# Turning the gathered rows of the last two experts on VectorE instead of TensorE in an attention and mixture-of-experts kernel

## The chip, the cores and the metric

The kernel runs on one core of one Trainium2 chip. A core has five engines that work side by side and wait for each other through semaphores: TensorE (PE in the profile; PEld is its weight load), VectorE (DVE), ScalarE (ACT), GpSimd (POOL) and SyncE (SP, which here only issues DMAs). Every engine takes its own instructions strictly in order. The metric is the time of one execution on the device in microseconds (us).

## What is computed

```python
# attention with a sigmoid: 8 batches, 12 heads, 448 tokens, 64 wide
scores = scale * np.matmul(q, k.transpose(0, 1, 3, 2)) - np.log(S)
x = np.matmul(1 / (1 + np.exp(-scores)), v)      # -> x: 3584 tokens x 768
# routing: each expert takes 448 tokens, by falling logit over all tokens and experts
logits = x @ w_gate                              # 3584 x 8
for idx in np.argsort(-logits.flatten()):
    tok, e = idx // E, idx % E
    if assigned[tok] >= 0 or counts[e] >= cap: continue
    assigned[tok] = e; counts[e] += 1
# experts: 768 -> 1024 -> 768
for e in range(E):
    h = np.maximum(x[mask] @ w1[e], 0.0)
    out[mask] = h @ w2[e]
```

All inputs and the output are float32.

## The kernel before

The program has two stages. In the first, attention is computed for 48 head pairs and the rows of x are stored to DRAM (`xs`). A row is not stored in the order of its 768 features. It is stored as four quarters of 192: quarter a holds, for each of the six blocks of 128 features, the 32 features that stand at place 32a to 32a+31 of the block.

In the second stage the eight experts run one after the other (`moe`). They are numbered here by the order in which the routing finishes them, 0 to 7. The first layer of an expert has four blocks of two weight units each, the second has three blocks of two, so an expert has 14 units; unit u of the whole program belongs to expert u // 14. TensorE multiplies in float32r, and each float32 operand is split in a high part, rounded by ScalarE (`xh`, `wh`, `hh`), and a low part that is the rest (`xl`, `wl`, `hl`). Three matmuls then replace one (lines 1000, 1002, 1004 in the first layer, 1037, 1039, 1041 in the second). An expert is 144 + 144 such matmuls of 448 columns; below they are counted 0 to 287.

Who makes the parts: ScalarE makes `wh` (L856) and GpSimd `wl` (L858), except that VectorE makes `wl` of the odd units from number 84 on. Of the first layer's output, ScalarE makes `hh` (L1008) and a plain copy into `yt` (L1011), and GpSimd makes `hl` from the two (L1012).

How x gets in: the 448 rows of an expert are gathered from `xs` by four indirect DMAs on the GpSimd queue (`gather`, L878, 128 rows each, the last 64). ScalarE puts each block of rows into the order of features (`order`, L887), and TensorE turns it by 24 small matmuls against the identity, in eight groups of three (`xturn`, L904). ScalarE and VectorE then make `xh` (L907) and `xl` (L908). This is done for an expert while the one before it runs.

The routing runs on VectorE (`Router`), one expert or two ahead of the matmuls. Its longest part is `grid_search`: nine rounds of three counts over a tile of keys (L321), each round needing the threshold `r_base` (L361) of the round before. After the ninth round TensorE turns `r_base` (L408) and sums the counts (L409), in line with its other matmuls. Then follow `place` (L452 to L461), `lists` (L481 to L496) and `remove`.

What sets the order: the program counts a clock of its own, 189 ns for each large matmul, and emits the other work between matmuls by due times on this clock. Each part of the routing has a time after which its next part is emitted, and `chores` is a list of due times with at most one chore per 1000 ns. Scatters of an expert's result (L956, on the GpSimd queue) and the stores and loads that bring the result into rows are chores as well. The engines then run freely in the order so written.

Of the kernel before, what the change touches and what calls it, by code (L numbers as in the profile page):

```python
# [7 lines left out]
F32 = mybir.dt.float32  # L8
F32R = mybir.dt.float32r
BF = mybir.dt.bfloat16  # L10
I32 = mybir.dt.int32
I16 = mybir.dt.int16
F16 = mybir.dt.float16
AF = mybir.ActivationFunctionType
OP = mybir.AluOpType
# [3 lines left out]
STEP = 4.0e36  # L19
BIG = 16384.0  # L20
TWO23 = float(2 ** 23)
XR_BUFS = 12
LATE = 1
XT_BUFS = 3
XZ_BUFS = 2
# [5 lines left out]
T_LATER = 1000  # L31
SLACK = 150
CHORE_NS = 1000
H_POOL = 8
EARLY = 1
FIRST = 4000.0
W_DVE = 84
Y_WAIT, Y_LATE = 5000, 26000
N_FAST = 9
PAD = 168  # L40
NONE = 1.0e30
FOUND, FOUND_ALL = 0x43E00000, 0x455FC800
# [14 lines left out]
def route_consts(nc, cp, K):  # L57

    K.G = cp.tile([128, 128], BF, name="c_G")
    ti = cp.tile([128, 128], I32, name="c_ti")  # L60
    nc.gpsimd.iota(ti, [[1, 128]], base=128, channel_multiplier=-1)
    t1 = cp.tile([128, 128], I32, name="c_t1")
    nc.gpsimd.iota(t1, [[1, 128]], base=0, channel_multiplier=0)
    t9 = cp.tile([128, 1], I32, name="c_t9")
    t10 = cp.tile([128, 1], F32, name="c_t10")
    nc.gpsimd.iota(t9, [[0, 1]], base=0, channel_multiplier=1)
    K.CN = cp.tile([128, 32], F32, name="c_CN")
    nc.gpsimd.memset(K.CN, 0.0)
    K.TRI = cp.tile([128, 128], BF, name="c_TRI")
    K.ones = cp.tile([128, 1], BF, name="c_ones")  # L70
    nc.gpsimd.memset(K.ones, 1.0)

    K.io64 = cp.tile([112, 64, 32], I16, name="c_io64")
    nc.gpsimd.iota(K.io64, [[1, 64], [0, 32]], base=0, channel_multiplier=0)
    K.io8 = cp.tile([112, 8], I16, name="c_io8")
    nc.gpsimd.iota(K.io8, [[1, 8]], base=0, channel_multiplier=0)

    K.rank = cp.tile([128, 8], F32, name="c_rank")
    t3 = cp.tile([128, 8], I32, name="c_t3")
    nc.gpsimd.iota(t3, [[-1, 8]], base=8, channel_multiplier=0)  # L80
# [12 lines left out]
    nc.gpsimd.iota(t6, [[1, 2], [2, 4]], base=0, channel_multiplier=0)

    K.kk = cp.tile([128, 16, 3], I32, name="c_kk")
    t8 = cp.tile([128, 3], I32, name="c_t8")
    nc.gpsimd.iota(t8, [[1, 3]], base=1, channel_multiplier=0)
    K.c0 = cp.tile([128, 3], I32, name="c_c0")
    for i, u in enumerate((0xBFFFFFFF, 0x00000000, 0x40000000)):
        nc.gpsimd.memset(K.c0[:, i:i + 1], _s32(u))  # L100
    yield
    yield
    nc.vector.tensor_scalar(t1, t1, 4, None, OP.logical_shift_right)
    nc.vector.tensor_scalar(t9, t9, 4, None, OP.logical_shift_right)
    nc.vector.tensor_copy(t10, t9)
    yield
    nc.vector.tensor_scalar(K.G, t1, t10, None, OP.is_equal)
    nc.vector.tensor_scalar(K.TRI, ti, 128.5, None, OP.is_gt)
    yield
    nc.vector.tensor_copy(K.rank, t3)  # L110
    nc.vector.tensor_copy(K.tok, t4)
    nc.vector.tensor_scalar(t5, t5, 31, None, OP.bitwise_and)
    t7 = cp.tile([128, 1], F32, name="c_t7")
    nc.vector.tensor_copy(t7, t5)
    yield
    nc.vector.tensor_scalar(K.SEL, t6, t7, None, OP.is_equal)
    g = 0
    for st in range(1, 16):
        sh = 30 - 2 * st
        nc.vector.tensor_scalar(K.kk[:, st], t8, sh, _s32(g), OP.logical_shift_left, OP.bitwise_xor)  # L120
        g ^= (0x4B000000 << sh) & 0xFFFFFFFF
        if st % 5 == 0:
            yield
    K.gfin = _s32(g)
    K.cw = cp.tile([128, N_FAST + 1, 3], F32, name="c_cw")
    for r in range(N_FAST + 1):
        nc.vector.tensor_scalar(K.cw[:, r], t8, 4.0 ** -r, None, OP.mult)


class Router:  # L130
# [335 lines left out]
    def lists(self, k):  # L466

        nc, K, wk, sl = self.nc, self.K, self.wk, self.sl
# [24 lines left out]
        for h in range(2):  # L493
            nc.tensor.matmul(p[64 * h:64 * h + 64, :4], bt, K.SEL[:, h, :], start=True, stop=True)
        idx = wk.tile([128, 4], I32, name="r_idx", bufs=8)
        nc.vector.tensor_scalar(idx, p[:, :4], 1792.0, None, OP.add)  # L496
        self.idx = idx

    def remove(self):

# [44 lines left out]
def moe_attention(tc, q, k, v, w_gate, w1, w2, out):  # L545
    nc = tc.nc
# [6 lines left out]
    with contextlib.ExitStack() as ctx:  # L553
# [248 lines left out]
        R.start(LE)  # L802
        late.pop(0)()
        late.pop(0)()
        picked, listed = {}, {}

        def routing():
            for kx in range(E):
                for t in R.phase(kx):
                    if kx not in picked and R.ei is not None:  # L810
                        picked[kx] = R.ei
                    yield t
                listed[kx] = R.idx
                R.ei = None
                yield 0

# [59 lines left out]
        def gather(kx, j, n):  # L876
            t = xg[kx, j] = xp.tile([128, DM], F32, name="xr", bufs=XR_BUFS)
            nc.gpsimd.indirect_dma_start(out=t[:n], out_offset=None, in_=xs,  # L878
                                         in_offset=bass.IndirectOffsetOnAxis(ap=listed[kx][:n, j:j + 1], axis=0))

        def order(kx, j, n):

# [207 lines left out]
        for kx in range(E):  # L1090
# [2 lines left out]

            def prepare():
                t0 = clock[0]
                lag = max(ORDER + 5000, min(14000, start + 40000 - t0))
                for j, n in blocks():
                    if kx:
                        chores.append((t0 + 1500 * j, kx + 1, lambda j=j, n=n: gather(kx + 1, j, n)))
                    else:  # L1100
                        gather(1, j, n)
                bl = list(blocks())
                hold.update({"from": t0 + lag - HOLD_NS, "left": 2 * len(bl)})

                def turn_x(j, n, hf):
                    xturn(kx + 1, j, n, hf, False)
                    hold["left"] -= 1
                chores.append((t0 + lag - ORDER, kx + 1, lambda: order(kx + 1, *bl[0])))
                for i, (j, n) in enumerate(bl):
                    def first(i=i, j=j, n=n):  # L1110
                        turn_x(j, n, 0)
                        if i + 1 < len(bl):
                            order(kx + 1, *bl[i + 1])
                    chores.append((t0 + lag + 1500 * j, kx + 1, first))
                    chores.append((t0 + lag + 1500 * j, kx + 1, lambda j=j, n=n: turn_x(j, n, 1)))
# [55 lines left out]
```

## Time and profile before

| | |
|---|---|
| median of 3 runs | 836.25 us (835.22 to 837.65) |
| profiled execution, its time | 836.41 us |
| profiled execution, its span | 834.6 us, so 1.8 us lie around the span |
| instructions | 15042 |
| HBM | read 105.02 MB, written 32.57 MB |

Rows of the timeline read: start in us from the start of the span, duration in us, engine, line, operation, output<-input, partitions x elements, count, and in square brackets the time for which the engine had stood idle and what ended that. Rows of a group read: count, then shortest, median and longest duration in ns, then first and last start in us. A matmul's recorded duration (0.37 us for 448 columns) is longer than its spacing (0.20 us), since matmuls are pipelined; the spacing is what counts for the time.

### The profile page before, as it was taken

How to read it: one execution, taken by the hardware profiler on the slowest of the kernel's cores; microseconds unless marked ns; L12 is line 12 of the kernel's file. 1: busy time of each engine (PE TensorE's matmuls, PEld its weight loads, DVE VectorE, ACT ScalarE, POOL GpSimd, SP SyncE). 2: the span in 40 equal slices, each digit the busy share in tenths (PEclk: the TensorE clock that was granted, in tenths of full speed). 3: DMA queues.
4: the chain of work that ended last, by engine and by line, in shares of the span. 5: the costliest groups of instructions: out<-in, count | busy, mean ns of one | idle time of the engine just before them, and what ended most of it. 6: DMA issues, size and time to landing. Idle time of an engine off the chain costs nothing.

```text
span 834.6 us, 15042 instructions
## 1 busy us (share of the span) xinstructions
PE 803.4 (96%) x5169; PEld 617.6 (74%) x5169; DVE 485.3 (58%) x1444; ACT 410.4 (49%) x509; POOL 463.5 (56%) x447
## 2 busy tenths in 40 slices
PE   6999999999999679999999999999999999999996
PEld 3454554445544469899899879889898889899996
DVE  4667666676668577468568558459468432241241
ACT  6777777787778234243343343432443342641421
POOL 9744444444430036746966854864784784481651
PEclk9999999999999889999999999999999999999998
DMA  8887777878772353357566566466565576745734
GB/s 171 169 179 159 172 177 153 181 151 173 172 141 72 105 180 100 98 167 216 166 181 199 177 194 180 143 205 178 151 221 160 158 234 173 216 152 142 226 121 133
DMA packets 259705, 138.71 MB, mean 166 GB/s; under 512 B 187136, under 2 KB 248832, under 8 KB 259616
## 3 DMA queue, kind: packets, MB, share of 16 engines
q1 hardware_dynamic: 246880, 104.14, 49.2%
q0 software_dynamic: 10880, 33.28, 12.9%
q8 instruction: 41, 0.67, 0.3%
q10 hardware_dynamic: 1856, 0.23, 0.2%
q14 instruction: 48, 0.39, 0.2%
HBM read 105.02 MB, written 32.57 MB: 165 GB/s over the span
## 4 chain that ended last, share of the span: by engine, by line
PE 54%; DVE 5%; issue 2%; DMA 1%; ACT 1%; POOL 1%; SPq 0%; POOLq 0%; DVEq 0%; ACTq 0%
PE sc L1000 9%; PE sc L1004 9%; PE sc L1002 9%; PE sc L1039 8%; PE sc L1037 8%; PE sc L1041 8%; PE tp L904 2%; DVE r_junk L321 2%; PE rt L487 1%; PE rt L1071 1%; DMA xr<-ys 1%; DMA xr<-xs,r_idx 1%; POOL out_dram L956 0%; DVE yt L934 0%; POOL wl L858 0%
## 5 line engine op out<-in xcount | busy, mean ns | idle before, releaser
L858 POOL TENSOR_TENSOR wl<-wr,wh 128x768 fp32r<-128x768 f32 (+1 forms) x96 | 203.3, 2129 | 66.4 <-ACT wh L856 66.1
L589 POOL DMA_DIRECT2D nkq<-in_q_dram x188 | 118.2, 643 | 114.2 <-DVE kqT L614 98.2
L629 ACT ACTIVATE at<-sc,bias 128x896 f32<-128x896 f32 x168 | 161.6, 1004 | 40.4 <-PE sc L639 24.3
L1041 PE MATMUL sc<-hh,wl 128*128 128x448 f32 (+2 forms) x400 | 146.2, 366 | 0.0
L1037 PE MATMUL sc<-hh,wh 128*128 128x448 f32 (+2 forms) x400 | 145.3, 363 | 0.4 <-ACT yt L969 0.4
L1000 PE MATMUL sc<-xh,wh 128*128 128x448 f32 (+2 forms) x396 | 145.3, 367 | 0.2 <-ACT xh L907 0.2
L1004 PE MATMUL sc<-xh,wl 128*128 128x448 f32 (+2 forms) x396 | 145.5, 367 | 0.0
L1039 PE MATMUL sc<-hl,wh 128*128 128x448 f32 (+2 forms) x400 | 145.1, 363 | 0.0
L1002 PE MATMUL sc<-xl,wh 128*128 128x448 f32 (+2 forms) x396 | 144.9, 366 | 0.0
L856 ACT ACTIVATE wh<-wr 128x768 fp32r<-128x768 f32 (+1 forms) x112 | 101.3, 937 | 73.6 <-PE sc L1039 55.1
L1012 POOL TENSOR_TENSOR hl<-yt,hh 128x896 fp32r<-128x896 f32 x32 | 68.2, 2131 | 99.9 <-ACT yt L1011 99.7
L663 PE MATMUL tp<-at,nv 128*64 128x448 f32 x576 | 118.8, 547 | 0.0
L1008 ACT ACTIVATE hh<-sc 128x896 fp32r<-128x896 f32 x32 | 29.4, 919 | 151.2 <-PE sc L1004 151.2
L623 DVE TENSOR_TENSOR kqL<-kqT,kqH 128x896 fp32r<-128x896 f32 (+1 forms) x49 | 52.5, 1072 | 52.3 <-ACT kqH L622 52.1
L1037 PEld LDWEIGHTS sc<-hh,wh 128*128 128x128 f32 x400 | 77.6, 194 | 4.4 <-ACT yt L969 0.6
L663 PEld LDWEIGHTS tp<-at,nv 128*64 128x64 f32 x576 | 37.2, 136 | 58.9 <-issue 56.4
L1000 PEld LDWEIGHTS sc<-xh,wh 128*128 128x128 f32 x396 | 76.0, 192 | 6.5 <-ACT xh L907 0.4
L1002 PEld LDWEIGHTS sc<-xl,wh 128*128 128x128 f32 x396 | 75.9, 192 | 6.4 <-issue 0.2
L1039 PEld LDWEIGHTS sc<-hl,wh 128*128 128x128 f32 x400 | 77.6, 194 | 4.1 <-issue 0.4
L1004 PEld LDWEIGHTS sc<-xh,wl 128*128 128x128 f32 x396 | 75.8, 191 | 6.0
L1041 PEld LDWEIGHTS sc<-hh,wl 128*128 128x128 f32 x400 | 77.6, 194 | 3.5
L639 PE MATMUL sc<-kqH 64*128 64x448 f32 x288 | 59.8, 412 | 7.2 <-ACT kqH L622 7.2
(232 smaller groups left out, 1077.3 us busy)
## 6 DMA issues: line engine op xcount, KB each, us to landing
wr<-in_moe_w_dram SPq DMA_DIRECT2D x64, 384.0 KB
wr<-in_moe_w_dram SPq DMA_DIRECT2D x48, 512.0 KB
nkq<-in_k_dram SPq DMA_DIRECT2D x192, 56.0 KB
nkq<-in_q_dram POOLq DMA_DIRECT2D x188, 56.0 KB, 2.8
ys<-yt SPq DMA_DIRECT2D x92, 112.0 KB
xs<-xz SPq DMA_DIRECT2D x28, 336.0 KB
nv<-in_v_dram SPq DMA_DIRECT2D x92, 96.0 KB
xr<-ys SPq DMA_DIRECT2D x21, 384.0 KB
```

Of the source, the lines that this page charges most:

```text
L589: qn.dma_start(t[o:o + 32, n], rws[x])
L629: nc.scalar.activation(a, p[:, :, :S], AF.Sigmoid, bias=bias, scale=1 / math.sqrt(D))
L663: nc.tensor.matmul(p[j * 64:j * 64 + 64, :S], nat["v", b, g][:, h0 + j, c, :], AT[b, pr, c][:, j, :], start=(c == 0), stop=(c == 2 and pr ...
L856: nc.scalar.activation(hi, raw[u], AF.Copy)
L858: eng.tensor_tensor(lo, raw[u], hi.bitcast(F32), OP.subtract)
L1000: nc.tensor.matmul(ph[:, f, lo:hi], wh[:, a, fs], xh[:, dd, lo:hi], start=st, stop=False)
L1002: nc.tensor.matmul(ph[:, f, lo:hi], wh[:, a, fs], xl[:, dd, lo:hi], start=False, stop=False)
L1004: nc.tensor.matmul(ph[:, f, lo:hi], wl[:, a, fs], xh[:, dd, lo:hi], start=False, stop=en)
L1012: nc.gpsimd.tensor_tensor(h2, h0, h1.bitcast(F32), OP.subtract)
L1037: nc.tensor.matmul(py[:, d2, :w], wh[:, a, dsl], h1, start=st, stop=False)
L1039: nc.tensor.matmul(py[:, d2, :w], wh[:, a, dsl], h2, start=False, stop=False)
L1041: nc.tensor.matmul(py[:, d2, :w], wl[:, a, dsl], h1, start=False, stop=(j == 1 and a == 3))
```

## The change

For experts 6 and 7 (`X_DVE = 6`) the rows are gathered in quarters. The list of tokens is also written out as 16 columns of 128 indices (`r_parts`): partition 32a+t of a column holds four times the row of a token plus a, so that one indirect DMA brings quarter a of 32 tokens to partitions 32a to 32a+31. Fourteen such DMAs bring the 448 tokens (`gather_parts`). VectorE then turns one feature block of all tokens at once, 14 blocks of 32 by 32 in each quarter (`turn_parts`), into PSUM; ScalarE makes `xh` and VectorE `xl` from there. No `order` and no TensorE turning is left for these two experts. The 16 columns cost TensorE eight more tiny matmuls for each list.

Besides, `hl` of experts 5, 6 and 7 is made by VectorE straight from PSUM (`H_POOL` 8 to 5; that branch of the code is there already), without the copy of ScalarE and the subtraction of GpSimd. `W_DVE` goes from 84 to 70: VectorE makes `wl` of the odd units from 70 on, which adds expert 5's seven. Buffers of gathered and result rows go from 12 to 8, and a pad from 168 to 120.

```diff
-XR_BUFS = 12
+XR_BUFS = 8
...
-H_POOL = 8
+H_POOL = 5
...
-W_DVE = 84
+W_DVE = 70
...
-PAD = 168
+PAD = 120
...
+X_DVE, PACE = 6, 1200
...
+    nc.vector.tensor_scalar(t11, t11, 5, None, OP.logical_shift_right)
+    nc.vector.tensor_scalar(K.quarter, t11, 4 * 1792.0, None, OP.add)
...
         idx = wk.tile([128, 4], I32, name="r_idx", bufs=8)
+        if k >= X_DVE:
+            for a in range(4):
+                for h in range(2):
+                    nc.tensor.matmul(p[32 * a:32 * a + 32, 16 + 8 * h:24 + 8 * h], bt[:, 32 * h:32 * h + 32],
+                                     K.SEL.rearrange("p h c -> p (h c)"), start=True, stop=True)
         nc.vector.tensor_scalar(idx, p[:, :4], 1792.0, None, OP.add)
-        self.idx = idx
+        self.idx = idx, None
+        if k >= X_DVE:
+            parts = wk.tile([128, 16], I32, name="r_parts")
+            nc.vector.tensor_scalar(parts, p[:, 16:32], 4.0, K.quarter, OP.mult, OP.add)
+            self.idx = idx, parts
...
+        def gather_parts(kx, i):
+
+            if i == 0:
+                xg[kx] = xp.tile([128, S // 32, DM // 4], F32, name="xz", bufs=1)
+            c = 8 * (i % 2) + i // 2 % 2 * 4 + i // 4
+            nc.gpsimd.indirect_dma_start(out=xg[kx][:, i, :], out_offset=None, in_=xs.rearrange("n (a c) -> (n a) c", a=4),
+                                         in_offset=bass.IndirectOffsetOnAxis(ap=parts[kx][:, c:c + 1], axis=0))
+
+        def turn_parts(kx, r):
+
+            if r == 0:
+                XH[kx] = (xp.tile([128, ND, S], F32R, name="xh", bufs=2),
+                          xp.tile([128, ND, S], F32R, name="xl", bufs=2))
+            xh, xl = XH[kx]
+            p = ps_t.tile([128, 512], F32, name="tp")[:, :S]
+            nc.vector.transpose(p.rearrange("p (i t) -> p i t", t=32), xg[kx][:, :, 32 * r:32 * r + 32])
+            nc.scalar.activation(xh[:, r, :], p, AF.Copy)
+            nc.vector.tensor_tensor(xl[:, r, :], p, xh[:, r, :].bitcast(F32), OP.subtract)
...
             def prepare():
                 t0 = clock[0]
+                if kx + 1 >= X_DVE:
+                    pace = min(2200, max(PACE, (start + 54000 - t0 - 17000) / (S // 32)))
+                    for i in range(S // 32):
+                        chores.append((t0 + pace * i, kx + 1, lambda i=i: gather_parts(kx + 1, i)))
+                    for r in range(ND):
+                        chores.append((t0 + pace * (S // 32) + 6500 + 1300 * r, kx + 1, lambda r=r: turn_parts(kx + 1, r)))
+                    return
```

Three places of the program show how instructions move. Rows of the changed kernel have its own line numbers.

The first place is VectorE in expert 5's first layer, in the grid search of expert 6, between the seventh round's `r_base` and the ninth round. Before, the eighth round follows the seventh at once, and the ninth the eighth:

```order
L361 TENSOR_SCALAR r_base<-r_acc,c_kw,r_base 128x1
L321 TENSOR_SCALAR r_junk,c_CN<-r_KE,r_T 128x224 x3
L326 STREAM_TRANSPOSE r_ct<-c_CN 128x32
L351 TENSOR_SCALAR rt<-c_kw,r_base 128x3
L329 TENSOR_REDUCE r_s_9449<-r_ct 128x2
L330 STREAM_TRANSPOSE r_ct<-r_s_9449 128x32
L356 TENSOR_SCALAR r_j_9447,r_acc<-r_ct 128x3
L359 SCALAR_TENSOR_TENSOR r_T<-r_acc,c_kw,rt 128x3
L361 TENSOR_SCALAR r_base<-r_acc,c_kw,r_base 128x1
L321 TENSOR_SCALAR r_junk,c_CN<-r_KE,r_T 128x224 x3
```

The same rounds in the changed kernel:

```order
L367 TENSOR_SCALAR r_base<-r_acc,c_kw,r_base 128x1
L873 TENSOR_TENSOR wl<-wr,wh 128x768
L327 TENSOR_SCALAR r_junk,c_CN<-r_KE,r_T 128x224 x3
L332 STREAM_TRANSPOSE r_ct<-c_CN 128x32
L357 TENSOR_SCALAR rt<-c_kw,r_base 128x3
L335 TENSOR_REDUCE r_s_9454<-r_ct 128x2
L336 STREAM_TRANSPOSE r_ct<-r_s_9454 128x32
L362 TENSOR_SCALAR r_j_9452,r_acc<-r_ct 128x3
L365 SCALAR_TENSOR_TENSOR r_T<-r_acc,c_kw,rt 128x3
L367 TENSOR_SCALAR r_base<-r_acc,c_kw,r_base 128x1
L1048 SCALAR_TENSOR_TENSOR hl<-sc,hh 128x896
L327 TENSOR_SCALAR r_junk,c_CN<-r_KE,r_T 128x224 x3
```

`wl` of unit 73 now stands ahead of the eighth round and `hl` of expert 5's first block ahead of the ninth; `wl` of unit 71 has come in, in the same way, between the fourth round and the fifth.

The second place is GpSimd from the end of expert 5's first layer through its second. Before, from the last `hl` on (L878 is a gather for expert 6, L956 a scatter of expert 4's result, L955 a one-element memset ahead of each scatter):

```order
L1012 TENSOR_TENSOR hl<-yt,hh 128x896
L858 TENSOR_TENSOR wl<-wr,wh 128x1024
L878 DMA xr<-xs,r_idx 128x768
L955 MEMSET spacer 1x1
L956 DMA out_dram<-xr,r_idx 3584x768
L955 MEMSET spacer 1x1
L956 DMA out_dram<-xr,r_idx 3584x768
L878 DMA xr<-xs,r_idx 64x768
L858 TENSOR_TENSOR wl<-wr,wh 128x1024
L955 MEMSET spacer 1x1
L956 DMA out_dram<-xr,r_idx 3584x768
L858 TENSOR_TENSOR wl<-wr,wh 128x1024 x2
```

The same stretch in the changed kernel, with L901 a gather of quarters (two of them, and the first scatter, stand ahead of these rows):

```order
L873 TENSOR_TENSOR wl<-wr,wh 128x1024
L901 DMA xz<-xs,r_parts 128x192
L989 MEMSET spacer 1x1
L990 DMA out_dram<-xr,r_idx 3584x768
L989 MEMSET spacer 1x1
L990 DMA out_dram<-xr,r_idx 3584x768
L901 DMA xz<-xs,r_parts 128x192
L989 MEMSET spacer 1x1
L990 DMA out_dram<-xr,r_idx 3584x768
L901 DMA xz<-xs,r_parts 128x192 x3
L873 TENSOR_TENSOR wl<-wr,wh 128x1024
L901 DMA xz<-xs,r_parts 128x192 x7
```

Four gathers have become 14, the `hl` and every second `wl` are gone, and half of the gathers stand behind the second `wl`, that of unit 82.

The third place is VectorE at the end of expert 5. Before, it makes `xl` of expert 6 from what TensorE has turned, between the steps that bring expert 5's result out of PSUM (L934):

```order
L908 TENSOR_TENSOR xl<-tp,xh 128x3x128 x6
L908 TENSOR_TENSOR xl<-tp,xh 128x3x64
L934 STREAM_TRANSPOSE yt<-sc 128x2x448
L908 TENSOR_TENSOR xl<-tp,xh 128x3x64
L858 TENSOR_TENSOR wl<-wr,wh 128x768
L934 STREAM_TRANSPOSE yt<-sc 128x2x448
L858 TENSOR_TENSOR wl<-wr,wh 128x768 x2
```

In the changed kernel two pairs of turning (L911) and low part (L913) stand ahead of these rows, and the other four are here; L968 is the last block of expert 5's result:

```order
L873 TENSOR_TENSOR wl<-wr,wh 128x768
L911 STREAM_TRANSPOSE tp<-xz 128x448
L913 TENSOR_TENSOR xl<-tp,xh 128x448
L911 STREAM_TRANSPOSE tp<-xz 128x448
L913 TENSOR_TENSOR xl<-tp,xh 128x448
L911 STREAM_TRANSPOSE tp<-xz 128x448
L913 TENSOR_TENSOR xl<-tp,xh 128x448
L968 STREAM_TRANSPOSE yt<-sc 128x2x448
L911 STREAM_TRANSPOSE tp<-xz 128x448
L913 TENSOR_TENSOR xl<-tp,xh 128x448
L873 TENSOR_TENSOR wl<-wr,wh 128x768
```

VectorE now does the turning itself, alternates with ScalarE for each of the six feature blocks, and has the last of expert 5's result to bring out ahead of the sixth.

More of the change, by code (lines that the diff above doesn't have):

```diff
@@ L87, in route_consts @@
     nc.gpsimd.memset(K.mv, 0.0)
+    K.quarter = cp.tile([128, 1], F32, name="c_q")
+    t11 = cp.tile([128, 1], I32, name="c_t11")
+    nc.gpsimd.iota(t11, [[0, 1]], base=0, channel_multiplier=1)
     K.SEL = cp.tile([128, 2, 4], F16, name="c_SEL")
@@ L804, in moe_attention @@
         late.pop(0)()
-        picked, listed = {}, {}
+        picked, listed, parts = {}, {}, {}
         def routing():
@@ L812, in routing @@
                     yield t
-                listed[kx] = R.idx
+                listed[kx], parts[kx] = R.idx
                 R.ei = None
```

## The prediction

> **What bounds the kernel now.** The page of the profile first: busy times and the chain of work that ended last.
>
> ```profile
> PE 803.4 (96%) x5169; PEld 617.6 (74%) x5169; DVE 485.3 (58%) x1444; ACT 410.4 (49%) x509; POOL 463.5 (56%) x447
> PE 54%; DVE 5%; issue 2%; DMA 1%; ACT 1%; POOL 1%; SPq 0%; POOLq 0%; DVEq 0%; ACTq 0%
> ```
>
> TensorE is the bound: the chain runs mostly over its lines. So an edit counts only by what it takes out of TensorE's stream, puts in, or makes it wait for. The group of line 1000 in two stretches gives the first layer of expert 6 and that of expert 7, which has no turning beside it.
>
> ```profile
> L1000 PE MATMUL sc<-xh,wh x48: 358/365/373, 702.5 to 735.8; 128*128 128x448 f32 x48
> L1000 PE MATMUL sc<-xh,wh x48: 362/365/369, 765.7 to 794.3; 128*128 128x448 f32 x48
> ```
>
> Expert 7: 28.6 us over 141 matmuls, 0.203 us each. Expert 6: 33.3 us. The difference, 4.7 us, is what turning expert 7's rows costs there.
>
> **What goes.** The timeline of TensorE around one group of three turnings of 128 rows, and one of 64:
>
> ```profile
> 681.95 0.36 PE L1039 MATMUL sc<-hl,wh 128*128 128x448 f32 x1
> 682.16 0.49 PE L904 MATMUL tp<-ident,xq 128*128 128x128 f32 x3
> ...
> 682.70 0.37 PE L1037 MATMUL sc<-hh,wh 128*128 128x448 f32 x1
> ...
> 691.28 0.37 PE L1039 MATMUL sc<-hl,wh 128*128 128x448 f32 x1
> 691.58 0.40 PE L904 MATMUL tp<-ident,xq 64*128 64x64 f32 x3
> 691.90 0.48 PE L1041 MATMUL sc<-hh,wl 128*128 128x448 f32 x1
> 692.22 0.37 PE L1037 MATMUL sc<-hh,wh 128*128 128x448 f32 x1
> ```
>
> From 681.95 to 682.70 are 0.75 us where two spacings take 0.41: a group of 128 rows costs 0.34. That of 64 rows costs 0.94 - 0.41 = 0.53. Six and two of them are 3.1 us for an expert. During expert 6 two waits come on top:
>
> ```profile
> 720.55 0.55 PE L904 MATMUL tp<-ident,xq 128*128 128x128 f32 x3 [1.04 <-ACT xq L887]
> 732.12 0.40 PE L904 MATMUL tp<-ident,xq 64*128 64x64 f32 x3 [0.31 <-DVE xl L908]
> ```
>
> 3.1 + 1.04 + 0.31 agrees with the 4.7 within 0.3. All of it goes: **-3.1 in expert 5, -4.7 in expert 6, -7.8 us**. The copies, subtractions and `order` that leave ScalarE and GpSimd give nothing: only those two waits were on them.
>
> **What comes in on TensorE.** Sixteen tiny matmuls; the nearest are the 32 of line 487:
>
> ```profile
> 661.97 0.37 PE L1000 MATMUL sc<-xh,wh 128*128 128x448 f32 x1
> 662.27 1.11 PE L487 MATMUL rt<-r_oh,c_mv 112*32 112x64 f16 x32
> 663.31 0.47 PE L1002 MATMUL sc<-xl,wh 128*128 128x448 f32 x1
> ```
>
> 1.34 - 0.20 us for 32 is 0.036 each: **+0.6 us** for 16.
>
> **The first new wait: the search of expert 6 on VectorE.** VectorE's timeline (the fourth round's first count, right behind the last `xl` of expert 5, and the ninth round's `r_base`) and what TensorE does with the last:
>
> ```profile
> 628.76 0.43 DVE L321 TENSOR_SCALAR_CACHE_REDUCE r_junk<-r_KE,r_T 128x224 bf16<-128x224 f32 x1
> ...
> 644.12 0.27 DVE L361 TENSOR_SCALAR r_base<-r_acc,c_kw,r_base 128x1 f32<-128x1 f32 x1
> ```
> ```profile
> 644.45 0.32 PE L408 MATMUL rt<-ident,r_base 128*128 128x128 f32 x1 [0.15 <-DVE r_base L361]
> ```
>
> TensorE already waits 0.15 us there: the six rounds run back to back and have no slack at all. The order of the changed kernel puts two `wl` and one `hl` among them, so every microsecond of these is a wait of TensorE, with the rest of expert 5 queued behind it. Their prices:
>
> ```profile
> 703.76 0.92 DVE L858 TENSOR_TENSOR wl<-wr,wh 128x768 fp32r<-128x768 f32 x1
> L934 DVE STREAM_TRANSPOSE yt<-sc 128x896 f32<-128x896 f32 x23 | 25.5, 1110 | 33.3 <-issue 21.6 <-PE sc L1041 6.9 <-POOL spacer L955 4.8
> ```
>
> `wl` alone 0.92; `hl` reads 896 columns of PSUM as line 934 does, 1.1. That is 2.9 us. But VectorE and GpSimd hinder each other:
>
> ```profile
> 713.24 1.55 DVE L858 TENSOR_TENSOR wl<-wr,wh 128x768 fp32r<-128x768 f32 x1 [8.55 <-ACT wh L856]
> 747.46 3.60 DVE L858 TENSOR_TENSOR wl<-wr,wh 128x1024 fp32r<-128x1024 f32 x1
> ```
> ```profile
> 636.02 1.85 POOL L858 TENSOR_TENSOR wl<-wr,wh 128x768 fp32r<-128x768 f32 x1 [3.04 <-ACT wh L856]
> ...
> 713.92 2.58 POOL L858 TENSOR_TENSOR wl<-wr,wh 128x768 fp32r<-128x768 f32 x1
> 747.55 2.41 POOL L858 TENSOR_TENSOR wl<-wr,wh 128x1024 fp32r<-128x1024 f32 x1
> ```
> ```profile
> 630.21 0.85 ACT L856 ACTIVATE wh<-wr 128x768 fp32r<-128x768 f32 x1 [1.02 <-issue]
> ```
>
> GpSimd needs 1.85 for a `wl` alone. With GpSimd beside it, VectorE's `wl` took 1.55 us when VectorE was 0.7 us ahead, and 3.60, until 1.1 us after GpSimd's end, when they began together. Unit 71's `wl` gets its turn after the fourth round, at 631.2 (a round is (644.4 - 628.8 - 1.1)/6 = 2.4 us, the 1.1 a line 934). GpSimd starts unit 72's at 631.1, as soon as the `wh` above is done, and is done 1.85 later. So I take 1.75 of blocking for unit 71 and none for unit 73, where GpSimd has nothing left to do: **+4.6 us** (2.9 to 4.6). [...]
>
> A smaller wait follows at the sums of `place`, for which VectorE had this room:
>
> ```profile
> 652.16 0.61 DVE L440 TENSOR_REDUCE rt<-r_w 112x32 f32<-112x256 f32 x1 [3.60 <-issue]
> ...
> 653.20 0.19 DVE L445 TENSOR_SCALAR csum<-csum,r_c 1x1 f32<-1x1 f32 x1
> ```
> ```profile
> 656.43 0.23 PE L458 MATMUL rt<-c_TRI,r_tot 64*112 64x64 bf16 x1
> ```
>
> Between 653.4 and 656.4 now come `wl`, `hl`, `wl` (2.9) and the 0.3 of `r_tot`: late by 0.2, with blocking by up to 2, and not at all if the unexplained idle 3.6 us does not come again. **+0.7 us** (0 to 1.5).
>
> **The second new wait: the start of expert 6.** Turning cannot begin before all 14 gathers have landed. GpSimd's rows of a scatter, a gather and a `wl`, the group of all gathers, the landing of all gathers and scatters, and when VectorE and ScalarE reach the start:
>
> ```profile
> 678.72 0.98 POOL L956 DMA_INDIRECT out_dram<-xr,r_idx  x1 [0.22 <-DMA wr<-in_moe_w_dram]
> 680.00 0.92 POOL L878 DMA_INDIRECT xr<-xs,r_idx  x1 [0.30 <-issue]
> 680.94 2.40 POOL L858 TENSOR_TENSOR wl<-wr,wh 128x1024 fp32r<-128x1024 f32 x1
> ```
> ```profile
> L878 POOL DMA_INDIRECT xr<-xs,r_idx x32: 903/960/1752, 290.4 to 704.4; - x32
> ...
> DMA to landing us min/median/max: 2.9/4.9/6.2
> ```
> ```profile
> 664.57 0.16 DVE L496 TENSOR_SCALAR r_idx<-rt 128x4 int32<-128x4 f32 x1 [0.91 <-PE rt L494]
> 668.00 0.92 ACT L1008 ACTIVATE hh<-sc 128x896 fp32r<-128x896 f32 x1 [5.25 <-PE sc L1004]
> ```
>
> A gather takes GpSimd 0.96 us and the 0.30 ahead of it. The one at 680.00 has 64 rows and takes 0.92, so size hardly matters, and I take 1.26 for a quarter gather (0.9 to 2.05, the group's ends, as bounds). In the times of before (all waits above shift both sides alike) the list is there at 665.2. Then 14 x 1.26 + 4 scatters x 1.3 + 2 `wl` x 2.4 = 27.6, and 1.3 for `wh` of unit 80, which is made behind the `hh` above: the last gather begins at 692.9 and lands, with 4.2 (2.9 to 5.4), at 697.1. [...]
>
> Then six times: VectorE turns, ScalarE makes `xh`, VectorE makes `xl`, one after the other.
>
> ```profile
> L908 DVE TENSOR_TENSOR xl<-tp,xh 128x384 fp32r<-128x384 f32 x45 | 24.8, 555 | 46.3 <-ACT xh L907 46.3
> 682.68 0.49 ACT L907 ACTIVATE xh<-tp 128x384 fp32r<-128x384 f32 x1 [8.16 <-PE tp L904]
> ```
>
> Turning 448 columns into PSUM is not in the trace; line 934 turns 896 out of PSUM in 1.1, and I take the half, 0.6 (0.5 to 1.1). With 0.54 and 0.62 for 448 columns of the other two and the hand-overs, a cycle is 1.85. Six are 11.1; `wl` of unit 85 between them with its `wh` 1.2, line 934 ahead of the sixth 1.1: done 13.4 later, at 710.5. TensorE would begin expert 6 at
>
> ```profile
> 702.52 0.36 PE L1000 MATMUL sc<-xh,wh 128*128 128x448 f32 x1
> ```
>
> less 3.1, plus 0.6: 700.0, and wants the sixth `xl` 25 matmuls later (it takes feature blocks 0 to 2 twice in 18 matmuls, then 3, 4, 5 by threes), at 705.1. **+5.4 us** (2.5 to 10). For expert 7 the gathers begin with expert 6 and have its whole first layer: no wait. The end of the kernel moves along unchanged. The fewer row buffers cost nothing: a gather takes one whose scatter was issued an expert earlier. Nor does `hl` on VectorE in experts 6 and 7, where no routing is left to delay and PSUM is held for `hh` and `hl` about as long as for two copies of ScalarE.
>
> **The sum:** -7.8 + 0.6 + 4.6 + 0.7 + 5.4 = +3.5 us on the profiled execution's 836.41 (its span 834.6 and 1.8 around), so 839.9; the median of the runs is 0.16 lower: **839.8 us**.
>
> **Rivals.** (a) The gathers are cheaper and the start is not late: at 0.94 us each they end when the code's due time for the first turning comes, matmul 250 of expert 5 (692.5; the list at matmul 127, then 14 x 1200 and 6500 ns at 189 each), and 0.8 us of wait remain. -1.1: 835.3. For it speaks their quarter of the bytes, against it the 64-row row. This is the one on the other side; it decides at 0.94 us a gather. (b) Unit 71's `wl` comes ahead of GpSimd, no blocking: 2.9 in place of 4.6 and 0 for 0.7, 837.4; the two starts are 0.1 us apart. (a) and (b) together: 832.9. (d) The gathers land in 2.9 us, the shortest of the row, since they are small: 838.5. [...] (c) Turning into PSUM at 1.1 us, or several gathers stretched towards the group's longest: +3 to +6 more, 843 to 846.
>
> **Chances.** Forecast (839 to 842.5) 0.42; (a) 0.17; (b) 0.13; (d) 0.08; (a) with (b), or a gain that I have not seen, 0.12; (c) 0.08. A measurement tells 0.3% from no change, 2.5 us, so faster is below 833.7 and slower above 838.8: faster 0.12 and a third of (a), 0.18; same the rest of (a), (b) and (d), 0.32; slower the forecast and (c), 0.50. The range goes from 832.5, (a) with (b), to 845.5, most of (c).
>
> **What would show it.** Right: a wait of 3 to 5 us of TensorE for `r_base` at the sum behind the search in expert 5; the first turning (`tp<-xz`) beginning within a microsecond of expert 6's first matmul or up to 5 us ahead, and waits of TensorE for `xh`, `xl` in the first 25 matmuls of expert 6, about 5 us in all; expert 6's first layer otherwise as short as expert 7's. Wrong: gathers below 1 us apart, or the turning done before expert 6 begins, or no wait at the search.

## The result: slower by 1.1%, and where the profile shows it

Changed kernel: 845.09 us median (844.95 to 846.18, 4 runs); the kernel before in the same session 836.13 us (835.22 to 837.65, 4 runs). The ratio is 1.011, 95% interval 1.0094 to 1.0126: 9 us slower, where 3.5 were forecast. The profiled execution has a span of 843.3 us against 834.6, and a mean granted clock of 0.981 against 0.989.

The page of the changed kernel, busy times and the chain that ended last by engine (lines have moved: 914 to 1075 are what was 880 to 1041, 414 was 408):

```profile
PE 803.6 (95%) x5137; PEld 616.5 (73%) x5137; DVE 512.0 (61%) x1475; ACT 394.3 (47%) x485; POOL 446.6 (53%) x449
PE 48%; DVE 7%; POOL 3%; DMA 3%; issue 2%; ACT 1%; SPq 0%; POOLq 0%; DVEq 0%; ACTq 0%
```

TensorE has 32 instructions fewer and is busy just as long. VectorE's part of the chain went from 5 to 7%, GpSimd's and the DMAs' from 1 to 3% each: the path now leaves TensorE in more places. The view of TensorE's waits from 640 us on (line waited at and releaser; us in total, times, longest):

```profile
PE rt L414 <- DVE r_base L367: 4.5, 1, 4.5
PE sc L1034 <- ACT xh L912: 4.0, 4, 1.6
...
PE sc L1036 <- DVE xl L913: 0.4, 2, 0.2
```

Both forecast waits are there. The first, in VectorE's timeline (start, duration, line; what stands in the search of expert 6) and in TensorE's:

```profile
631.32 2.58 DVE L873 TENSOR_TENSOR wl<-wr,wh 128x768 fp32r<-128x768 f32 x1
...
642.16 0.95 DVE L873 TENSOR_TENSOR wl<-wr,wh 128x768 fp32r<-128x768 f32 x1
...
645.47 1.08 DVE L1048 SCALAR_TENSOR_TENSOR hl<-sc,hh 128x896 fp32r<-128x896 f32 x1
648.60 0.27 DVE L367 TENSOR_SCALAR r_base<-r_acc,c_kw,r_base 128x1 f32<-128x1 f32 x1
```
```profile
648.93 0.47 PE L414 MATMUL rt<-ident,r_base 128*128 128x128 f32 x1 [4.52 <-DVE r_base L367]
...
649.99 0.57 PE L1034 MATMUL sc<-xh,wh 128*128 128x448 f32 x1
650.36 0.57 PE L1036 MATMUL sc<-xl,wh 128*128 128x448 f32 x1
...
654.84 0.41 PE L1036 MATMUL sc<-xl,wh 128*128 128x448 f32 x1
655.09 0.36 PE L1038 MATMUL sc<-xh,wl 128*128 128x448 f32 x1
655.29 0.37 PE L1034 MATMUL sc<-xh,wh 128*128 128x448 f32 x1
```

The 2.58 + 0.95 + 1.08 = 4.6 us are the sum that the prediction worked out, blocked `wl` and all, and the wait is 4.52. But look at the starts behind it: from 649.99 on matmuls follow each other at 0.373 us, and only from 655.09 at 0.203 again. The view of windows shows why: its column PEclk, the granted clock, is the first figure behind POOL's.

```profile
650.00:652.00 2.00, 2.00 (x7) 1.78 (x6) 0.75 (x5) 0.00 (x0) 0.00 (x0) 0.50 1.06 311
```

After the wait TensorE runs at half its clock for some 5 us. No view of waits lists that: the engine counts as busy.

The start of expert 6: GpSimd's first, slowest and last gathers, VectorE's first turning and sixth `xl`, and TensorE.

```profile
672.97 0.98 POOL L901 DMA_INDIRECT xz<-xs,r_parts  x1 [2.69 <-DVE ML L522]
...
679.41 3.73 POOL L901 DMA_INDIRECT xz<-xs,r_parts  x1 [0.16 <-issue]
...
688.52 1.72 POOL L901 DMA_INDIRECT xz<-xs,r_parts  x1 [0.30 <-issue]
...
702.86 0.95 POOL L901 DMA_INDIRECT xz<-xs,r_parts  x1 [0.30 <-issue]
```
```profile
706.28 0.37 PE L1075 MATMUL sc<-hh,wl 128*128 128x448 f32 x1
708.27 0.47 PE L1034 MATMUL sc<-xh,wh 128*128 128x448 f32 x1 [1.63 <-ACT xh L912]
...
719.34 0.47 PE L1034 MATMUL sc<-xh,wh 128*128 128x448 f32 x1 [0.77 <-ACT xh L912]
720.00 0.47 PE L1036 MATMUL sc<-xl,wh 128*128 128x448 f32 x1 [0.19 <-DVE xl L913]
```
```profile
706.98 0.66 DVE L911 STREAM_TRANSPOSE tp<-xz 128x448 f32<-128x448 f32 x1 [8.94 <-DMA xz<-xs,r_parts]
```

TensorE could have begun at 706.48 and come to the sixth `xl` 25 matmuls later, at 711.6; it gets there at 720.0. So the start loses 8.4 us. The granted clock is 0.50 here too, from 710 to 716 us, with six spacings of 0.37 us in a row, but at the end of the stretch TensorE waits for the sixth `xh` again (the 0.77): VectorE's sixth cycle sets this loss, and the slow matmuls lie inside it.

From the starts of the first matmul of each stage, in this execution against before (us):

| stretch | before | after | difference | forecast |
|---|---|---|---|---|
| expert 5, first layer | 32.97 | 39.76 | +6.8 | +5.6 |
| expert 5, second layer, to its last matmul | 34.3 | 31.4 | -2.9 | -2.8 |
| from there to expert 6's second layer | 34.1 | 37.9 | +3.9 | +0.7 |
| expert 6, second layer, to expert 7's | 58.47 | 58.47 | 0.0 | 0 |
| end, behind the last stage | | | +0.9 | 0 |

(The 0.6 of the tiny matmuls is halved between the first two rows, where the two lists are made.) The last row lies behind the issue of the last scatter, which is 7.75 us later than before (837.37 against 829.62), while the span ends 8.7 later. From that issue to the end of the span are 5.0 us in the kernel before, 5.9 in the changed one and in every kernel below with quarters for both experts, and 5.4 to 5.5 in those with quarters for expert 7 alone and in the one with the low parts alone. The traces show no instruction there; what makes the 0.9 us stays open.

### The profile page after: what moved, and what is told of

Read it like the earlier page. It is cut to its first block, busy times and chain, and to the rows that moved or that the text cites. A ratio compares the mean times of both kernels' runs of the same rounds, so it can differ in the third digit from the quotient of the medians.

```text
span 843.3 us, 14964 instructions
## 1 busy us (share of the span) xinstructions
PE 803.6 (95%) x5137; PEld 616.5 (73%) x5137; DVE 512.0 (61%) x1475; ACT 394.3 (47%) x485; POOL 446.6 (53%) x449
## 4 chain that ended last, share of the span: by engine, by line
PE 48%; DVE 7%; POOL 3%; DMA 3%; issue 2%; ACT 1%; SPq 0%; POOLq 0%; DVEq 0%; ACTq 0%
PE sc L1034 8%; PE sc L1036 8%; PE sc L1038 8%; PE sc L1073 7%; PE sc L1071 7%; PE sc L1075 7%; DVE r_junk L327 2%; POOL xz L901 2%; PE tp L938 1%; DMA xr<-xs,r_idx 1%; POOL out_dram L990 1%; DVE wl L873 1%; PE rt L493 1%; POOL wl L873 1%; DVE yt L968 1%
## 5 line engine op out<-in xcount | busy, mean ns | idle before, releaser
L873 POOL TENSOR_TENSOR wl<-wr,wh 128x768 fp32r<-128x768 f32 (+1 forms) x89 | 185.4, 2094 | 126.2 <-ACT wh L871 124.9
L1034 PE MATMUL sc<-xh,wh 128*128 128x448 f32 (+2 forms) x396 | 147.6, 373 | 4.2 <-ACT xh L912 4.0
L1036 PE MATMUL sc<-xl,wh 128*128 128x448 f32 (+2 forms) x396 | 147.0, 371 | 0.4 <-DVE xl L913 0.4
L1046 POOL TENSOR_TENSOR hl<-yt,hh 128x896 fp32r<-128x896 f32 x20 | 42.7, 2133 | 54.5 <-ACT yt L1045 43.1
```

Source lines behind the costliest of these rows:

```text
L873: eng.tensor_tensor(lo, raw[u], hi.bitcast(F32), OP.subtract)
L1034: nc.tensor.matmul(ph[:, f, lo:hi], wh[:, a, fs], xh[:, dd, lo:hi], start=st, stop=False)
L1036: nc.tensor.matmul(ph[:, f, lo:hi], wh[:, a, fs], xl[:, dd, lo:hi], start=False, stop=False)
```

## The experiments

**One part of the change alone: the low parts.** The kernel before, with

```
-H_POOL = 8
+H_POOL = 5
-W_DVE = 84
+W_DVE = 70
```

> The kernel of before with only the two moves of low parts (wl of odd units from 71 on and hl of experts 5 to 7 on VectorE); all x in rows, turned by TensorE. Theory A: the wait for r_base is there, 4 to 4.5 us, and the half clock of 2.4 us behind it; nothing is gained: 842 to 843.5 us. Theory B: the wait without the clock, 840.5 us. Theory C: as before, 836 us.

Measured 843.71 us (841.66 to 843.91), ratio 1.009 (1.0073 to 1.0107). The wait is 4.5 us, in a kernel without a single quarter gather; ten matmuls behind it are at 0.37 us. The low parts alone cost 7.8 of the 9 us by the medians (the profiled execution, 841.66, is the shortest of the four): what the quarters take from TensorE and what they cost at expert 6's start almost cancel.

**Quarters for expert 7 only.** The changed kernel with

```
-X_DVE, PACE = 6, 1200
+X_DVE, PACE = 7, 1200
-XR_BUFS = 8
+XR_BUFS = 10
```

(With the 12 row buffers of before, the pool `xp` would need 94.5 KB per partition where 89.5 are left; hence 10.)

> The changed kernel with only expert 7's x gathered in quarters; expert 6's comes in rows and is turned by TensorE (10 row buffers). Theory A (quarters are late for expert 6 only because 14 gathers, their landing and six cycles on VectorE have too little time between its list and its start): expert 7 loses nothing at its start, and the 8.5 us that expert 6 lost at its start go, of which its turnings take back about 3 in expert 5; the wait for r_base of 4.5 us and the half clock behind it stay. About 839.5 us. Theory C (quarters cost wherever they lie: they stretch GpSimd's and the queues' work): expert 7's start, or other transfers in expert 6, lose several us too: 842 us or more.

Measured 839.24 us (838.26 to 839.72), ratio 1.0035 (1.0023 to 1.0047). Its waits keep the first line and lose all that had to do with `xh` and `xl`:

```profile
PE rt L414 <- DVE r_base L367: 4.5, 1, 4.5
PE tp L1009 <- ACT yt L1003: 0.5, 1, 0.5
PE sc L1071 <- ACT yt L1003: 0.4, 1, 0.4
```

So quarters make no late start where an expert's whole first layer lies between list and use (they can cost elsewhere, as will be seen); the late start belongs to expert 6, whose first gather begins 33 us before TensorE is done with expert 5 (672.97 to 706.5 in the changed kernel).

**Filling the wait.** Does idle time make the clock drop? Twenty matmuls, whose results nothing reads, ahead of the transposition that waits (`self.fill` is expert 5's `xh`):

```
+FILL = 20
...
+        if k == 6:
+            for _ in range(FILL):
+                nc.tensor.matmul(p[:, :448], self.fill[:, 0, :128], self.fill[:, 0, :], start=True, stop=True)
         nc.tensor.transpose(p[:, :128], self.base.to_broadcast([128, 128]), K.ident)
```

> The changed kernel with 20 matmuls of 448 columns, whose results nothing uses, put ahead of the transposition that waits for r_base in expert 5: 4.1 us of work in the 4.5 us of the wait. Theory A: TensorE is no longer idle, the clock stays up, and 2.0 to 2.5 us go although work was added: about 842.7 us. Theory B (the drop is not made by the idle time): 845 us or somewhat more, with the same 14 matmuls at 0.37 us.

Measured 843.44 us (841.76 to 845.05; the changed kernel had 844.95 to 846.18), ratio 1.0092 (1.0073 to 1.0111). The ranges touch, so the total alone would be weak; the place is clear. TensorE's timeline, and the window behind:

```profile
642.65 4.29 PE L417 MATMUL rt<-xh 128*128 128x448 f32 x20
647.33 0.32 PE L418 MATMUL rt<-ident,r_base 128*128 128x128 f32 x1 [0.39 <-DVE r_base L368]
```
```profile
648.00:652.00 4.00, 4.00 (x22) 3.71 (x22) 0.96 (x6) 0.00 (x0) 0.00 (x0) 1.00 1.07 292
```

With 4.3 us of useless work in the same gap, the clock stays at 1.00 and not one matmul behind it is slow. Expert 5's first layer takes 38.5 us instead of 39.8: the half clock is gone, and two waits of 0.4 us each, for a `wl` and for the `r_tot` of `place`, have appeared.

**The wait alone.** The kernel before, with four (or, `WAIT = 12`, twelve) more counts on VectorE whose results nothing reads:

```
+WAIT = 4
...
+            if k == 6 and not more:
+                for _ in range(WAIT):
+                    self.count(base, K.CN[:, 31:32])
             nb = wk.tile([128, 1], F32, name="r_base")
```

> The kernel of before with four more counts on VectorE (1.5 us, their results are not used) ahead of expert 6's last r_base: a wait of TensorE of 1.6 us and nothing else new. Theory A, with what the 2.8 us wait of the first set showed (ten matmuls at half clock): 1.6 us is too short, the clock stays up, +1.5 us. Theory A2 (every wait of over a microsecond is followed by some microseconds at half clock): 8 to 14 matmuls at 0.37 us, +3 to +4 us.

> The kernel of before with twelve more counts on VectorE (4.4 us, results not used) ahead of expert 6's last r_base: a wait of 4.5 us as the changed kernel has, with nothing else of the change. Theory A: the wait, and 9 to 14 matmuls at 0.37 us behind it: +6 to +7 us, 842 to 843 us. Theory B (the drop of the clock belongs to the moved low parts and not to the wait): +4.4 us, 840.3 us, no matmul at 0.37.

With four: 838.65 us in one run. With twelve: 844.4 us (843.8 to 844.95), ratio 1.0096 (1.0076 to 1.0116); a count cost 0.47 us, so the wait was longer than meant. TensorE with four, then with twelve:

```profile
646.03 0.32 PE L412 MATMUL rt<-ident,r_base 128*128 128x128 f32 x1 [1.85 <-DVE r_base L365]
```
```profile
650.39 0.47 PE L412 MATMUL rt<-ident,r_base 128*128 128x128 f32 x1 [5.79 <-DVE r_base L365]
...
651.45 0.57 PE L1004 MATMUL sc<-xh,wh 128*128 128x448 f32 x1
651.83 0.57 PE L1006 MATMUL sc<-xl,wh 128*128 128x448 f32 x1
...
656.30 0.52 PE L1006 MATMUL sc<-xl,wh 128*128 128x448 f32 x1
```

Nothing of the change is in this kernel, and the drop is there. Set side by side (length of expert 5's first layer from its first matmul to the second layer's first; before: 32.97 with a wait of 0.15):

| kernel | wait, us | spacings of 0.37 us in a row | stage longer by | of that beyond the wait |
|---|---|---|---|---|
| four counts | 1.85 | 0 | 1.7 | 0.0 |
| units 71 and 73 on GpSimd (next) | 2.80 | 9 | 4.3 | 1.5 |
| low parts alone | 4.51 | 9 | 5.9 | 1.5 |
| changed kernel | 4.52 | 13 | 6.8 | 2.3 |
| quarters for expert 7 only | 4.52 | 14 | 6.8 | 2.4 |
| twelve counts | 5.79 | 14 | 8.2 | 2.6 |

(The last column is net of the 0.15 us of before and, in the two rows with quarters for expert 6, of 0.16 us for its eight tiny matmuls.) A slow spacing costs 0.17 us more than a usual one, so 9 make 1.5 and 14 make 2.4. A wait of 1.85 us cost itself; those of 2.8 us or more cost 1.5 to 2.6 us on top. Equal waits of 4.5 us were followed by 9 or by 13 to 14 slow spacings, so the extra is not a function of the wait's length alone. (Both rows of 9 are from the shortest of their kernels' four executions; the others were up to 2.5 us longer and have no trace.) Three waits of kernels further down add to the rows: after 1.61 us no spacing is slow, after 2.09 us 8 are, after 2.52 us 7. Of all these waits the shortest with slow spacings behind it was 2.09 us, and the longest without them 1.85 us.

**Which low part makes the wait?** The changed kernel with

```
-W_DVE = 70
+W_DVE = 74
```

> The changed kernel with the low parts of weight units 71 and 73 on GpSimd again; all else as changed. Theory A (the wait of TensorE for r_base is made by the two wl and the hl, and the half clock that follows is the price of the wait's length): the wait falls from 4.5 us to about 1 us, too short for a drop of the clock, so the half clock behind it (14 matmuls at 0.37 instead of 0.20 us, 2.4 us) goes as well: 5.5 to 6 us less than the changed kernel, about 839.3 us. Theory B (the drop of the clock in that stage has another cause than the wait, such as the load of the other engines): the wait falls alike, the clock stays down: 3.5 us less, about 841.6 us. Theory C (the slowdown comes only from the gathers in quarters): no change, 845 us.

Measured 842.43 us (841.91 to 844.42), ratio 1.0082 (1.0064 to 1.01). The forecast of 1 us of wait was wrong: 3.5 us of `wl` went and the wait fell by only 1.7. VectorE's timeline and TensorE's:

```profile
642.90 1.09 DVE L1048 SCALAR_TENSOR_TENSOR hl<-sc,hh 128x896 fp32r<-128x896 f32 x1 [1.56 <-ACT hh L1042]
...
646.03 0.27 DVE L367 TENSOR_SCALAR r_base<-r_acc,c_kw,r_base 128x1 f32<-128x1 f32 x1
```
```profile
646.36 0.32 PE L414 MATMUL rt<-ident,r_base 128*128 128x128 f32 x1 [2.80 <-DVE r_base L367]
```

Without the `wl` ahead of it, `hl` reaches its turn before TensorE has finished expert 5's first block, and VectorE stands for 1.56 us until ScalarE has made `hh`. A round of the search that is queued behind an `hl` waits for TensorE, and TensorE then waits for the round: 1.56 + 1.09 = 2.65 us, which the 2.80 agrees with.

**The search freed of both.** As above, and expert 5's `hl` on GpSimd again:

```
-H_POOL = 5
+H_POOL = 6
-W_DVE = 70
+W_DVE = 74
```

> The changed kernel with units 71 and 73's wl and expert 5's hl on GpSimd again, so that the search of expert 6 on VectorE is free of both; hl of experts 6 and 7 and wl of odd units from 75 on stay on VectorE. Theory A: no wait for r_base over 0.3 us and no half clock there; the start of expert 6 still loses about 8.5 us, since its list and TensorE come earlier by the same time: 836.0 - 7.8 + 0.6 + 8.5 = 837.3 us. Theory D (the loss at the start of expert 6 is made by the wait before it, which throws the emission of the gathers and the engines out of step): the start loses 5 us or less, 834 us or less. If GpSimd with four more hl of 2.1 us is late with the gathers, up to 841 us.

Measured 841.6 us (841.36 to 842.75), ratio 1.0064 (1.0045 to 1.0082). The wait for `r_base` is back at 0.16 us, but VectorE's later work, two `wl` in a row ahead of the sums of `place`, now shows:

```profile
PE rt L464 <- DVE r_tot L460: 1.1, 1, 1.1
PE sc L1038 <- DVE wl L873: 0.8, 1, 0.8
PE rt L458 <- DVE r_ei L535: 0.7, 1, 0.7
```

The wait for `r_tot` ends 2.7 us behind the one for `wl` (658.17 and 655.48), and 6 spacings at 0.37 us follow it. With the third wait the stage is still 4.4 us longer than before, which is the size of that forecast's miss. The start of expert 6 loses 8 us as in the changed kernel, with a shorter wait ahead of it: the second loss is not a consequence of the first.

**Quarters without the moves of low parts.** All low parts as before; first with quarters for expert 7 only (`X_DVE` 7 and 10 row buffers, as above), then for both experts:

```
-H_POOL = 5
+H_POOL = 8
-W_DVE = 70
+W_DVE = 84
```

> The kernel of before with one thing of the change: expert 7's x in quarters, turned by VectorE; low parts as before, expert 6 in rows (10 row buffers). Theory A (what the change costs is only the search's wait with its clock and the late start of expert 6; the turnings taken from TensorE are a real gain): no wait for r_base, the 4.7 us of expert 6's first layer go and 0.3 us of tiny matmuls come: 831.5 us. Theory E (the turnings were mostly hidden and taking them away gives nothing): 835 to 836 us.

> The changed kernel with all low parts as before (odd wl on VectorE from unit 84 on only, every hl on GpSimd); quarters for experts 6 and 7. Theory A: no wait for r_base, but GpSimd has three wl of 2.4 us and one or two hl of 2.1 us more among the gathers, less what VectorE's wl stretched them by: the last gather begins 6 to 8 us later against TensorE than in the changed kernel, and the start of expert 6 loses 12 to 15 us: 836 - 7.2 + 13.5 = about 842 us. Theory C (what the start loses is set by VectorE's turning or by the landing, not by GpSimd's row of work): 8 us there, 837 us.

For expert 7: 836.78 us (835.06 to 838.22), ratio 1.0006 (0.9996 to 1.0016), no difference. For both: 848.73 us (848.01 to 849.29), ratio 1.016 (1.0144 to 1.0175). Both forecasts were too low, for one reason that the prediction had not thought of. GpSimd's timeline with quarters for expert 7, and TensorE's:

```profile
729.88 1.36 POOL L901 DMA_INDIRECT xz<-xs,r_parts  x1 [0.30 <-issue]
731.26 2.12 POOL L1046 TENSOR_TENSOR hl<-yt,hh 128x896 fp32r<-128x896 f32 x1
733.33 2.35 POOL L873 TENSOR_TENSOR wl<-wr,wh 128x1024 fp32r<-128x1024 f32 x1
```
```profile
735.73 0.74 PE L1075 MATMUL sc<-hh,wl 128*128 128x448 f32 x1 [2.52 <-POOL wl L873]
736.27 0.57 PE L1071 MATMUL sc<-hh,wh 128*128 128x448 f32 x1
```

Five gathers in a row (724.85 to 731.24) and an `hl` stand ahead of a `wl` that TensorE needs at 733.2. From expert 6's second layer to expert 7's first are 33.8 us instead of 29.3: the wait of 2.52 us, and seven spacings of 0.37 us in a row behind it, take back most of what the turnings gave. With quarters for both experts the same kind of wait has this line, and the first of the three, in expert 5's second layer, these rows:

```profile
PE sc L1075 <- POOL wl L873: 6.0, 3, 3.7
```
```profile
697.93 0.48 PE L1075 MATMUL sc<-hh,wl 128*128 128x448 f32 x1 [2.09 <-POOL wl L873]
...
699.12 0.57 PE L1071 MATMUL sc<-hh,wh 128*128 128x448 f32 x1
699.49 0.57 PE L1073 MATMUL sc<-hl,wh 128*128 128x448 f32 x1
```

Eight spacings of 0.37 us follow this wait of 2.09 us, and eight the longest. The start of expert 6 lost 7.4 us there and not the 12 to 15 of the forecast, so that term was wrong as well.

So fourteen gathers do not fit on GpSimd beside the low parts of before. The low parts that the change moves to VectorE make room for them, and there they meet the search.

**Room on GpSimd for expert 6.** Low parts of `wl` from unit 79 on, `hl` from expert 6 on; and

```
-... (Y_LATE if kx < E - 2 else 4 * wait) ...
+... (50000 if kx == 4 else Y_LATE if kx < E - 2 else 4 * wait) ...
...
-if t >= t_route and (not hold["left"] ...
+if t >= t_route and not (kx == 5 and 6 in listed or kx == 6 and t < start + 6000) and (not hold["left"] ...
```

> The changed kernel with room made on GpSimd's row of work for expert 6: wl of odd units on VectorE only from 79 on, expert 5's hl on GpSimd (so the search and the sums of place are free), the scatters of expert 4 behind the gathers, the routing of expert 7 held until expert 6 has begun (so that its 2.28 us r_oh does not lie beside a gather). Theory A: no wait of over 1 us in expert 5, the last gather begins near 692 us and lands near 696, all spaced at 1.25 us but for wl and hl between; the sixth xl is done near 709, and the start of expert 6 loses 4 to 5 us: about 833 us. Theory F (gathers are stretched by the other loads of the queues and not by VectorE or their neighbours): gathers of over 1.7 us again, 836 us or more.

Measured 843.1 us (842.28 to 844.34), ratio 1.009 (1.0076 to 1.0104): a miss by 10 us. The gathers did begin from 667.39 to 691.82 as worked out, but the first turning came at 697.72, 5.9 us behind the last gather's begin and not 4 (sixth `xl` begun at 710.08), TensorE waited 1.6 us for a GpSimd `wl` in expert 5, and waits of 0.9, 0.6 and less came at the start of expert 7, whose list had been held back. Four things were changed at once and the losses moved, so the time decides nothing between A and F. Two gathers still took 1.78 and 1.66 us; the rows beside them, which speak against F, are taken up below.

**What is left when each low part goes where nothing waits.** Quarters for expert 7, `hl` of experts 6 and 7 on VectorE (no search runs there any more), `wl` as before; and, as a control, only this `hl` in the kernel before:

```
-X_DVE, PACE = 6, 1200
+X_DVE, PACE = 7, 1200
-H_POOL = 5
+H_POOL = 6
-W_DVE = 70
+W_DVE = 84
-XR_BUFS = 8
+XR_BUFS = 10
```

> As the kernel with quarters for expert 7 alone and the low parts of before, but hl of experts 6 and 7 on VectorE, where no search runs any more. Theory A (that kernel lost its 4.4 us of gain to one wait of 2.5 us for a wl that stood behind five gathers and an hl of 2.1 us on GpSimd, and to the half clock behind it): without the hl on GpSimd, four of 2.1 us in expert 6, the wl is made in time, no wait of over 0.6 us is left but the two of before: about 831.8 us. Theory G (VectorE's four hl and six turnings now make TensorE wait): waits for hl or xl, 834 us or more.

> The kernel of before with hl of experts 6 and 7 on VectorE and nothing else of the change. Theory A: these hl were hidden on either engine and no search waits behind them: 835 to 836 us, no difference that can be told. If this kernel is faster by 2 us or more, a gain of the kernel with quarters for expert 7 belongs to hl and not to the quarters.

Measured 832.67 us (831.38 to 833.29) against 836.65 us, ratio 0.9955 (0.9941 to 0.9968): faster than both kernels. The control: 835.8 us (834.69 to 836.85), ratio 0.9993 (0.9984 to 1.0002), no difference that can be told. So the gain needs the quarters. All waits of TensorE from 600 us on in the faster kernel:

```profile
PE tp L1009 <- ACT yt L1003: 0.5, 1, 0.5
PE sc L1071 <- ACT yt L1003: 0.4, 1, 0.4
PE rt L415 <- DVE r_junk L327: 0.2, 1, 0.2
PE rt L414 <- DVE r_base L367: 0.2, 1, 0.2
```

From expert 5's second layer to expert 6's second layer it needs 63.8 us where before needed 68.4: the 4.6 us of turning expert 7's rows.

## Why the prediction was right in direction and wrong in size

The direction and both new waits were forecast. What failed are two terms of the sum: the first wait had no term for the half clock behind it (2.3 us), and the second took each of the 14 gathers at 0.96 us, though VectorE's own instructions held two of them up (3.0 us, most of it this); 0.9 us at the end of the span stays unexplained. By its own steps, in the order of the sum:

- **-7.8 for the turnings, +0.6 for sixteen tiny matmuls**: right. Expert 5's second layer is 2.9 us shorter where -3.1 + 0.3 was taken; the kernels with quarters for expert 7 show the other part by itself, 4.6 us less with eight tiny matmuls where -4.7 + 0.3 was taken. The tiny matmuls cost half of the forecast (a list of expert 6 takes 0.28 us of TensorE's stream, 671.08 to 671.36, where it took 0.12).
- **+4.6 for the first new wait**: the wait was right to 0.1 us, with the blocking of unit 71 (2.58 us for 0.92). Wrong was what the step left out: a term for the clock. The sum priced each wait at its own length, and this one cost 2.3 us more at half clock. Filling the gap with 4.29 us of matmuls removed the drop (clock 1.00), and a bare wait of 5.79 us in the kernel before made it (14 spacings of 0.37 us).
- **Every microsecond of these is a wait of TensorE**: true in the changed kernel and not in general. With the `wl` gone, `hl` itself waits for TensorE's first block, so the three prices do not add: without 3.5 us of `wl`, 1.7 us of wait went.
- **+0.7 for the sums of `place`**: came out as nothing, since TensorE was late by the first wait anyway. Where that wait was taken away, 1.1 us of it appeared.
- **+5.4 for the second new wait**: the mechanism was right, the size 8.4. The landing (4.1 us against 4.2) and the 13.4 us of six cycles (13.0 measured) held, the landing in part by luck: the row that it was taken from mixes gathers (4.4 to 6.2 by themselves) with scatters (2.9 to 3.9), so that 4.2 was below every gather of before, and the 2.9 of rival (d) is a scatter's. The row of GpSimd's work did not hold: it was worked out as 27.4 us from the first gather to the last, 692.9 - 665.5, and took 29.9. Two of the fourteen gathers took 3.73 and 1.72 us where I took 0.96 for each (+3.5), and the 1.3 us taken for `wh` of unit 80 did not come. The group of the gathers before had a longest of 1.75, which the range kept as rival (c), but not one of 3.73. The list came 0.6 us later than the waits ahead explain, and TensorE 0.4 us earlier.

The sum by these measurements: +6.8 - 2.9 + 3.9 + 0.9 = +8.7, by which the span grew. So +3.5 became +8.7 by +2.3 (clock), +3.0 (start of expert 6), +0.9 (end), -0.7 (`place`), -0.3 (tiny matmuls) and -0.2 for the first wait, net of the 0.15 us that was there before; 0.2 is left. The signs named beforehand were there: a wait of 3 to 5 us for `r_base`, the first turning 1.3 us ahead of expert 6's first matmul, 4.4 us of waits for `xh` and `xl`. Of the rivals (a), (b) and (d) are refuted by rows (gathers are 1.25 us apart; unit 71 was blocked; the last gather took 4.1 us to land); (c), 843 to 846, holds the time, but only its stretched gathers were there, and they are about half of what was missing; the turning took 0.66 us and not 1.1. That the range reached as far as the measured time is therefore partly luck: nothing in it stood for the clock or for the end.

What stretched the two gathers can be read from the rows. VectorE's, beside the two of the changed kernel:

```profile
678.87 2.28 DVE L487 TENSOR_TENSOR r_oh<-c_io,rt 112x2048 f16<-112x2048 int16 x1
681.07 1.22 DVE L873 TENSOR_TENSOR wl<-wr,wh 128x1024 fp32r<-128x1024 f32 x1
...
688.20 1.18 DVE L873 TENSOR_TENSOR wl<-wr,wh 128x1024 fp32r<-128x1024 f32 x1
```

The longer gather began at 679.41, inside `r_oh`, and ended at 683.14, 0.85 us behind the end of the `wl`; the other began at 688.52, inside a `wl`, and ended 0.86 us behind it. The same holds elsewhere: in the 14 profiles, from 600 us on, 69 gathers and scatters took over 1.1 us. Each began inside a `wl` or `r_oh` on VectorE and ended 0.81 to 0.88 us behind the end of that instruction, or of the one that followed it at once; a gather alone took 0.95. Those that began ahead of a `wl`, or together with it, took their usual time. It does not take quarters: the kernel with the low parts alone has the same pair beside a gather of 128 whole rows,

```profile
678.54 3.73 POOL L878 DMA_INDIRECT xr<-xs,r_idx  x1
```

and the kernel with quarters for both experts and the low parts of before, where no `wl` of expert 5 is on VectorE, has none over 0.98 us among the gathers of expert 6. The prediction had seen that VectorE and GpSimd hinder each other (its rows of VectorE's `wl`: 0.92 us alone and 1.55 beside GpSimd's with 768 columns, 3.60 beside it with 1024), but applied it to `wl` alone and not to the gathers. No run moves only the VectorE instruction beside a gather, so this rests on the rows and not on an experiment made for it.

## What to carry to other kernels

Price a wait of the engine that is the bound at more than its length: here a wait of 1.85 us cost itself, one of 2.8 us or more 1.5 to 2.6 us on top (and one of 2.09 us was followed by 8 slow matmuls), which no list of waits shows and the starts of the matmuls behind it do. When work is moved to an engine with idle time, read what is queued behind it there and who waits for that: VectorE had 42% idle and no slack in the search, and its `wl` held up GpSimd's gathers; GpSimd had 44% idle and no room for five gathers ahead of a `wl`. A change in several parts is worth taking apart: the part that pays here (expert 7's quarters, and `hl` where no search runs) was hidden under two that cost.

## What the runs showed of the hardware that was not expected

- TensorE at half clock (spacing 0.373 us for 448 columns where 0.203 is usual; granted clock 0.50 in the changed kernel, 650 to 654 us) after single waits of 2.09, 2.52, 2.80 us and more, and after two of 0.8 and 1.05 us within 3.5 us; none after single waits of 1.61 and 1.85 us. It lasted 2.2 to 5.2 us (6 to 14 spacings).
- An indirect gather took GpSimd 0.95 us with a quarter of a row per partition and 0.96 us with a whole one (medians), and 3.73 us in five kernels when it began inside VectorE's `r_oh` with a `wl` behind that: each of the 69 gathers and scatters that took over 1.1 us began inside a `wl` or `r_oh` on VectorE and ended 0.81 to 0.88 us behind it.
- VectorE turned 448 columns into PSUM in 0.66 us, a little over half of the 1.11 us that 896 columns out of PSUM took.
